# Two ordering edges and one moved load at the hand-over from attention to the first GLU layer

## Chip, cores and metric

One core of a Trainium2 chip; each ratio compares runs of one chip. The metric is the time of one execution on the device in microseconds (us), median of several.

## The reference, cut to what matters

```python
x = A_x                                             # 2048 tokens x 1024, bf16
x = x + _A_ref(_layernorm(x), A_wqkv, A_wo)         # dilated local attention, 32 heads of 32, window 8
x = x + _B_ref(_layernorm(x), W_gate, W_up, W_down) # relu(x Wg) * (x Wu) @ Wd, 3584 wide
x = x + _A_ref(...); x = x + _B_ref(...)            # the same again
```

## The kernel before: the parts that matter here

The 2048 tokens are worked in 4 blocks of 512, twice, so 8 block steps `n`. TensorE should never wait; VectorE does the attention of a later block while TensorE does the big matmuls of an earlier one. The argument is about one place: attention of block 0 ends, and layer B of block 0 begins. In that stretch TensorE does, in this order, V of blocks 1 and 2 (`acc_v`), the output projection of block 0 (`acc_wo`), V of block 3 (`acc_v`), then the gate and up products of layer B (`acc_g`, `acc_u`).

What must happen between `acc_wo` and `acc_g` for each of the four 128-token tiles t of block 0: VectorE evicts `acc_wo` into x, the tile is normalized (t=0 and 1 on ScalarE, t=2 and 3 on VectorE, the power -0.5 on POOL, the GpSimd engine), and a DMA transpose turns it into `xnT_b`, which every `acc_g` reads whole.

```python
def ln2(n, ats, turn_at=None, dve=()):            # norm in front of layer B
    stats, apply, turn, hold = ln_steps(n, "b", False, dve)
    for t, a in enumerate(ats):
        ev.append((a, stats[t]))
        ev.append((a + 4.0, apply[t]))
        if turn_at is None:
            ev.append((a + 6.5, turn(t)))         # DMA transpose of tile t
    ...
ln2(0, [t_wo0 + 2 * GRP * (t + 1) + 0.1 for t in range(TPB)], None, (2, 3))
```

Events (time, function) are sorted by time and emitted in that order. The times are a plan, not a schedule: the compiler then orders each engine's instructions by itself, and an earlier event has priority. Only the DMAs and the groups of matmuls keep the emitted order, because `sp_dma` and `pe_group` chain each to the previous one with an ordering edge (`tc.issue_after`: an instruction is placed behind another). All DMAs but two loads of x at the start go through one queue.

Weights come in 1 MB slabs through a ring of 5 buffers. A load is emitted when the slab five places earlier in the plan is done:

```python
def slab_events(events):
    for i, (key, src, _) in enumerate(slab_plan):
        ...                                       # f: allocate from the ring, load
        events.append((slab_plan[i - RING][2] + 0.3 if i >= RING else 0.1 * i, f))
```

The plan's order is ..., V (2 slabs), wo (2), g0, u0, g1, u1, g2, ... (g for gate, u for up; these names are used below). The two wo slabs are planned to be done earlier than the two V slabs, so u1 and g2 are emitted before u0 and g1.

The attention of block 1 begins with sums of products q*k on VectorE, 16 products (`t`, the first of each half `ac`) and 14 adds, 2.2 us each:

```python
nc.vector.tensor_tensor(t[:], i0, i1, op=ALU.mult)   # 128 x 2048, f32 out
if c > 1: add(h, c - 1)
...
spread(sums1[:5], t_qk1 + 50.0, 4.4)                 # products 0..4
spread(sums1[5:], t_v3 + 6.0, 4.4)                   # the rest
```

## Time and profile before

Median 1647.76 us of three runs.

| What | Where it shows | us |
|---|---|---|
| TensorE busy | page | 1618.9 of 1646.7 (98%) |
| first acc_wo waits for oT | TensorE waits | 1.7 |
| acc_g waits (called "the pause" below) | TensorE waits | 6.2 |
| from the end of V of block 3 (151.0, where the next group would have started) to the second acc_g | timeline | 12.8, of which 3.45 is work |

The TensorE waits of the kernel before from 60 us to the end (engine, line, what it waited for: us in total, times, longest). These are all its waits in that stretch; the slow clock after the pause comes on top. `issue` means that the profile shows no releaser for the matmul itself; its weight load waited for `xnT_b` (PEld, 6.7 us in the view of that tile):

```profile
PE acc_g L115 <- issue: 6.2, 1, 6.2
PE acc_wo L115 <- DMA oT<-o_d: 1.7, 1, 1.7
PE acc_u L115 <- DMA w_u<-in_B_W_up_dram: 0.5, 1, 0.5
```

The same on the timeline of TensorE (start, duration, what, in brackets the idle time before it):

```profile
123.38 13.99 PE L115 MATMUL acc_wo<-w_o,oT 128*128 128x512 bf16 x62 [1.69 <-DMA oT<-o_d]
137.21 13.98 PE L115 MATMUL acc_v<-xnT_a,w_v 128*128 128x512 bf16 x64
157.38 3.57 PE L115 MATMUL acc_g<-xnT_b,w_g 128*128 128x512 bf16 x8 [6.20 <-issue]
161.48 2.50 PE L115 MATMUL acc_u<-xnT_b,w_u 128*128 128x512 bf16 x8 [0.52 <-DMA w_u<-in_B_W_up_dram]
163.81 1.89 PE L115 MATMUL acc_g<-xnT_b,w_g 128*128 128x512 bf16 x8
```

A group of 8 matmuls takes 1.89 us when all is well, starting every 1.73 us. After the pause the first takes 3.57: the clock is slow.

The DMA queue at the pause, from the timeline of SP (start, time that the issuing took):

```profile
140.31 6.57 SPq L104 DMA_TRANSPOSE xnT_b<-xn_b  x2
146.98 0.53 SPq L104 DMA_DIRECT2D w_u<-in_B_W_up_dram  x1
147.60 0.58 SPq L104 DMA_DIRECT2D w_g<-in_B_W_gate_dram  x1
148.28 7.04 SPq L104 DMA_TRANSPOSE xnT_b<-xn_b  x2
155.42 0.52 SPq L104 DMA_DIRECT2D w_u<-in_B_W_up_dram  x1
```

Here is what to see: transposes 0 and 1, then u1 and g2, then transposes 2 and 3, which took 7 us to issue, then u0, which acc_u waits for.

And VectorE, from its timeline. The first line is the product `ac`, which stands in front of the rest of the softmax of block 0; then the last attention output of block 0, the product just in front of the first eviction of acc_wo, that eviction, and the last norm (t=3):

```profile
79.09 2.28 DVE L411 TENSOR_TENSOR ac<-q,k 128x2048 f32<-128x2048 bf16 x1
...
117.06 0.76 DVE L476 TENSOR_TENSOR ohm<-pv 128x512 bf16<-128x512 bf16 x2
...
129.18 2.29 DVE L411 TENSOR_TENSOR t<-q,k 128x2048 f32<-128x2048 bf16 x1
131.39 1.28 DVE L518 TENSOR_TENSOR x<-acc_wo,x 128x512 bf16<-128x512 f32 x2
...
150.81 0.55 DVE L235 TENSOR_SCALAR xn_b<-x,mv,rstd 128x1024 bf16<-128x1024 bf16 x1 [0.44 <-POOL rstd L262]
```

### The profile page before, as it was taken

What the parts mean: (1) busy time and instruction counts of PE and PEld (TensorE: products, weight loads), DVE (VectorE), ACT (ScalarE), POOL (GpSimd) and SP (SyncE); (2) the same over time, 40 slices, a digit from 0 to 9 for tenths busy, and PEclk for the clock granted to TensorE, in tenths of its full rate; (3) what the DMA queues carried; (4) which work ended last, traced back from release to release, by engine and by line L of the source; (5) the groups of instructions that cost most, each with busy time, mean ns of one, the idle gap of its engine ahead of it and who ended that gap; (6) DMA issues with size and microseconds to landing.
All of it is one profiled execution on the core that took longest, in us unless ns stands there. A gap on an engine that the chain in (4) does not pass through costs nothing.

```text
span 1646.7 us, 18588 instructions
## 1 busy us (share of the span) xinstructions
PE 1618.9 (98%) x7527; PEld 777.7 (47%) x7576; DVE 1058.7 (64%) x918; ACT 511.9 (31%) x1057; POOL 267.0 (16%) x220
## 2 busy tenths in 40 slices
PE   7998999999999999999999999999999999999999
PEld 4543445444454445444454444544445444444444
DVE  3699898978198845949459493694927948211111
ACT  5834412414231522315124151340513411131110
POOL 1322005401052102111052010520105100000000
PEclk9999999999999999999999999999999999999999
DMA  9548766755747475774747748477475774655441
GB/s 295 93 141 229 181 169 189 204 171 164 219 148 208 133 208 156 225 207 142 210 155 203 188 153 230 157 185 204 151 228 178 190 220 151 203 154 183 153 163 68
DMA packets 371222, 296.81 MB, mean 180 GB/s; under 512 B 142400, under 2 KB 351296, under 8 KB 370240
## 3 DMA queue, kind: packets, MB, share of 16 engines
q1 hardware_dynamic: 370848, 295.10, 61.7%
q8 instruction: 59, 0.97, 0.2%
q10 hardware_dynamic: 288, 0.52, 0.1%
q14 instruction: 27, 0.22, 0.0%
HBM read 256.77 MB, written 21.00 MB: 169 GB/s over the span
## 4 chain that ended last, share of the span: by engine, by line
PE 90%; DVE 4%; ACT 3%; DMA 1%; issue 1%; POOL 1%; SPq 0%; ACTq 0%; DVEq 0%; POOLq 0%
PE acc_u L115 24%; PE acc_g L115 23%; PE dacc L115 23%; PE acc_wo L115 6%; PE acc_k L115 5%; PE acc_q L115 5%; PE acc_v L115 4%; DVE pv L473 1%; DMA x<-in_A_x_dram 1%; DVE t L411 1%; DVE pv L474 1%; ACT xn_a L221 0%; ACT xn_a L222 0%; DVE ac L421 0%; DMA w_u<-in_B_W_up_dram 0%
## 5 line engine op out<-in xcount | busy, mean ns | idle before, releaser
L115 PE MATMUL acc_g<-xnT_b,w_g 128*128 128x512 bf16 x1792 | 425.1, 380 | 6.2 <-issue 6.2
L115 PE MATMUL acc_u<-xnT_b,w_u 128*128 128x512 bf16 x1792 | 423.9, 379 | 0.5 <-DMA w_u<-in_B_W_up_dram 0.5
L115 PE MATMUL dacc<-w_d,hT 128*128 128x512 bf16 x1759 | 386.3, 379 | 1.7
L543 DVE TENSOR_TENSOR hT<-acc_u,r 128x512 bf16<-128x512 f32 x224 | 154.1, 690 | 317.4 <-PE acc_u L115 304.6
L542 ACT ACTIVATE r<-acc_g 128x512 bf16<-128x512 f32 x224 | 132.6, 594 | 704.9 <-PE acc_g L115 702.0
L115 PEld LDWEIGHTS <-w_g 128*128 128x128 bf16 x1792 | 175.0, 98 | 220.2 <-DMA xnT_b<-xn_b 6.7
L115 PEld LDWEIGHTS <-w_u 128*128 128x128 bf16 x1792 | 175.4, 98 | 213.1 <-DMA w_u<-in_B_W_up_dram 1.4
L115 PEld LDWEIGHTS <-hT 128*128 128x128 bf16 x1792 | 175.3, 98 | 211.4
L411 DVE TENSOR_TENSOR t<-q,k 128x2048 f32<-128x2048 bf16 x98 | 223.7, 2290 | 10.0 <-ACT k L354 7.0
L421 DVE TENSOR_TENSOR ac<-ac,t 128x2048 f32<-128x2048 f32 x84 | 192.0, 2286 | 0.4
L359 POOL COPY kh<-k 128x14 bf16<-128x14 bf16 x64 | 85.9, 1347 | 449.7 <-ACT k L354 449.7
L570 DVE TENSOR_TENSOR x<-dacc,x 128x512 bf16<-128x512 f32 x64 | 42.5, 688 | 164.6 <-PE dacc L115 164.6
L473 DVE TENSOR_TENSOR pv<-a,vhm 128x4096 bf16<-128x4096 bf16 x64 | 145.6, 2289 | 0.0
L226 POOL TENSOR_TENSOR st_b<-st_b,neg_half 128x1 f32<-128x1 f32 x30 | 62.7, 2095 | 325.2 <-ACT st_b L225 325.2
L115 PE MATMUL acc_wo<-w_o,oT 128*128 128x512 bf16 x496 | 111.0, 379 | 2.5 <-DMA oT<-o_d 1.7
L226 POOL TENSOR_TENSOR st_a<-st_a,neg_half 128x1 f32<-128x1 f32 x32 | 44.0, 1376 | 339.8 <-ACT st_a L225 339.8
L115 PEld LDWEIGHTS <-oT 128*128 128x128 bf16 x512 | 50.0, 98 | 62.2 <-DMA oT<-o_d 2.2
L474 DVE TENSOR_TENSOR pv<-pv 128x2048 bf16<-128x2048 bf16 x64 | 77.9, 1222 | 0.2
L358 POOL COPY k<-kh 128x14 bf16<-128x14 bf16 x48 | 67.5, 1406 | 53.4 <-DVE t L411 53.4
L221 ACT ACTIVATE xn_b<-x 128x1024 bf16<-128x1024 bf16 x30 | 31.3, 1045 | 93.9 <-DVE x L518 93.9
L350 ACT CAST q<-acc_q 128x512 bf16<-128x512 f32 x64 | 37.3, 583 | 68.5 <-PE acc_q L115 68.5
L315 ACT CAST vT<-acc_v 128x512 bf16<-128x512 f32 x64 | 36.9, 586 | 66.5 <-PE acc_v L115 66.5
(123 smaller groups left out, 1178.1 us busy)
## 6 DMA issues: line engine op xcount, KB each, us to landing
w_g<-in_B_W_gate_dram SPq DMA_DIRECT2D x56, 1024.0 KB, 6.4
w_u<-in_B_W_up_dram SPq DMA_DIRECT2D x56, 1024.0 KB, 5.2
w_d<-in_B_W_down_dram SPq DMA_DIRECT2D x48, 1024.0 KB, 5.8
w_o<-in_A_wo_dram SPq DMA_DIRECT2D x16, 1024.0 KB, 7.2
vhm<-v_d SPq DMA_DIRECT2D x32, 284.0 KB, 6.9
v_d<-vT SPq DMA_DIRECT2D x8, 1024.0 KB, 9.7
oT<-o_d SPq DMA_DIRECT2D x32, 256.0 KB, 4.2
w_d<-in_B_W_down_dram SPq DMA_DIRECT2D x16, 512.0 KB, 3.8
```

The source lines that it names most:

```text
L115: tail_pe[0] = nc.tensor.matmul(*args, **kwargs).ins
L226: nc.gpsimd.tensor_tensor(rstd, vpe, neg_half[:, 0:1], op=ALU.pow)
L350: nc.scalar.copy(q[:], acc[:])
L358: nc.gpsimd.tensor_copy(k[:, 0:HALO], khalo[n - 1][:, c, :])
L359: nc.gpsimd.tensor_copy(khalo[n][:, c, :], k[:, BLK:BLK + HALO])
L411: nc.vector.tensor_tensor(t[:], i0, i1, op=ALU.mult)
L421: nc.vector.tensor_tensor(o, ac[:], t[:], op=ALU.add)
L473: nc.vector.tensor_tensor(tt[:], a_bc, v_sh, op=ALU.mult)
L474: nc.vector.tensor_tensor(tt[:, 0:4], tt[:, 0:4], tt[:, 4:8], op=ALU.add)
L542: nc.scalar.activation(r[:], acc[:], ACT.Relu)
L543: nc.vector.tensor_tensor(hold["hT"][:, j, :], accs["u"][:], r[:], op=ALU.mult)
L570: nc.vector.tensor_tensor(xs, ac[t], xs, op=ALU.add)
```

## The change

Its intent: the products of block 1 shall not run in front of work that the hand-over waits for. Products 0 to 4 are held by an ordering edge behind the last attention output of block 0, and the rest behind the norm of t=3. The last transpose is emitted 1 us later and the others 0.5 us earlier, so that the load of u0 goes in front of the last one. The norm of block 3 is emitted 10 us later.

```diff
+    gate = [None]
@@ apply(t), norm on VectorE
-                    nc.vector.tensor_scalar(hold["xn"][:, t, :], ..., op0=ALU.subtract, op1=ALU.mult)
+                    gate[0] = nc.vector.tensor_scalar(hold["xn"][:, t, :], ..., op0=ALU.subtract, op1=ALU.mult).ins
@@ prod_sum_steps
-                nc.vector.tensor_tensor(t[:], i0, i1, op=ALU.mult)
+                if n == 1:
+                    with tc.issue_after(gate[0]):
+                        nc.vector.tensor_tensor(t[:], i0, i1, op=ALU.mult)
+                else:
+                    nc.vector.tensor_tensor(t[:], i0, i1, op=ALU.mult)
@@ pv_steps
-                nc.vector.tensor_tensor(ohm[:, ...], tt[:, 0], tt[:, 1], op=ALU.add)
+                gate[0] = nc.vector.tensor_tensor(ohm[:, ...], tt[:, 0], tt[:, 1], op=ALU.add).ins
@@ ln2
-                ev.append((a + 6.5, turn(t)))
+                ev.append((a + (7.5 if t == TPB - 1 else 6.0), turn(t)))
@@
-    ln1(3, 66.0, t_v2 + 9.5, True, 5.0)
+    ln1(3, t_qk1 + 12.0, t_v2 + 9.5, True, 5.0)
-    spread(sums1[5:], t_v3 + 6.0, 4.4)
+    spread(sums1[5:], t_v3 + 5.0, 4.4)
```

## The prediction

> **What bounds the kernel.** TensorE: 98% busy on the page, 90% of the chain that ended last. After the start-up its list of waits holds two losses that matter:
>
> - 1.69 us at 121.7 us: the first acc_wo waits for oT, the attention output read back (timeline of TensorE).
> - The pause at 151.0 us: V of block 3 is done, acc_g starts at 157.38 (6.2 us idle; the weight load waits for xnT_b, the normalized, transposed input). acc_g then takes 3.57 us instead of 1.89; acc_u waits 0.5 us for w_u. The granted clock was 0.60 in 157.4 to 164 (windows). The Trainium skill ("TensorE: Matmul & The Clock Gate", section "Part 1: The HAM clock gate") says the clock halves after an idle window of about 3.4 us; the trace agrees (about 2.5 us lost after this pause, none after the 1.69 us one). The second acc_g starts at 163.81; without the pause: 151.0 + 3.45 = 154.5. Loss 9.3 us.
>
> Together about 11 us, 0.7%.
>
> **What the change does.** Nothing is added or removed; VectorE order and DMA issue order change.
>
> 1. The first product (ac, 2.2 us at 79.09) stood before reciprocal, a and pv of block 0. Held behind the last pv it leaves pv 2.2 us earlier (end 117.7 to 115.5), and oT too: the 1.69 us pause goes.
> 2. Products 5 and on are held behind the last normalization on VectorE (t=3). It ran at 150.81; without two products and an add ahead of it I expect 142 to 145.
> 3. The load of the first w_u moves ahead of the last transpose in the one DMA queue. Issued at 155.42, landed 161.43; now issued near 147 to 150.
> 4. The norm of block 3, emitted 10 us later, already filled ScalarE's idle time: nothing.
>
> **How much is on the critical path.** The queue is the catch. In the trace two 1 MB loads (w_u, w_g at 146.98 and 147.60) go between transposes 1 and 2. Transpose 2, issued at 148.28, took 8.1 us to land, and transpose 3 landed right behind it at 157.35 although its input was ready at 151.36. So the pause was bounded by transpose 1, whose input comes from ScalarE's norm of t=1 (ready 145.6), plus 2.5 MB of queue. That norm hangs on the evictions of acc_wo and moves by only 2 to 4 us. A third 1 MB load, about 3 us at this window's 350 GB/s, now stands before transpose 3. So transpose 3 lands at 154 to 158 instead of 157.35; w_u no longer waits (0.5 to 1 us). The 1.7 us won at acc_wo partly become a longer pause. Net gain about 3 us; if the ScalarE norms come 5 us earlier, 8; if only 2, none.
>
> Later: the sums of block 1, wanted near 208.8, ended near 200; VectorE goes on with them in the pause, so they stay in time.
>
> **Prediction.** 1644.5 us, 8 in 10 within 1638.5 to 1649.0. Faster by over 2%: 0.01; within 2%: 0.98; slower: 0.01.
>
> **What would show it.** Timeline of VectorE: no ac between ssum and rs; pv ends near 115.5. TensorE waits: none of acc_wo for oT; acc_g still waits for xnT_b, 4 to 8 us, and starts cold; acc_u waits for nothing. The first w_u is issued before the last transpose. Second acc_g at 158 to 164.
>
> **What would make it wrong.** The compiler orders VectorE or ScalarE otherwise: acc_wo evicted at once would bring transposes 0 and 1 forward by 5 us or more, the queue would drain before V of block 3 ends, and nearly all 11 us would be won. Or the products held back come late for the logits at 208.8 and TensorE stalls there.

## The result, and the profile after

| Kernel | Median us | Runs | Ratio to before (95%) |
|---|---|---|---|
| before | 1648.04 | 4 | |
| after | 1650.80 | 4 | 1.0015 (0.9998 to 1.0032) |

Ratios here and below are the mean time of one kernel's runs over that of the other's of the same rounds, so not quite the ratio of the medians quoted. The sign is wrong: about 2.5 us slower (0.15%) where 3 us faster was predicted, and 1650.8 lies above the range that ended at 1649.0. The interval alone barely includes 1; the traces and the experiment e2 below settle the sign.

The TensorE waits of the kernel after, from 60 us to the end:

```profile
PE acc_g L118 <- issue: 11.0, 1, 11.0
PE acc_wo L118 <- DVE x L525: 0.2, 1, 0.2
```

The wait for oT and the wait for w_u are gone, as intended. The pause grew from 6.2 to 11.0 us. On the timeline of TensorE:

```profile
121.08 10.52 PE L118 MATMUL acc_wo<-w_o,oT 128*128 128x512 bf16 x48
...
135.26 14.17 PE L118 MATMUL acc_v<-xnT_a,w_v 128*128 128x512 bf16 x64
160.44 3.57 PE L118 MATMUL acc_g<-xnT_b,w_g 128*128 128x512 bf16 x8 [11.01 <-issue]
163.81 2.38 PE L118 MATMUL acc_u<-xnT_b,w_u 128*128 128x512 bf16 x8
166.02 1.89 PE L118 MATMUL acc_g<-xnT_b,w_g 128*128 128x512 bf16 x8
```

The second acc_g starts 2.2 us later than before (166.02 against 163.81), and the span is 2.2 us longer (1648.9 against 1646.7): everything after is the old trace, shifted. The DMA queue, timeline of SP:

```profile
139.99 6.57 SPq L107 DMA_TRANSPOSE xnT_b<-xn_b  x2
146.65 0.53 SPq L107 DMA_DIRECT2D w_u<-in_B_W_up_dram  x1
147.27 0.59 SPq L107 DMA_DIRECT2D w_g<-in_B_W_gate_dram  x1
147.96 4.41 SPq L107 DMA_TRANSPOSE xnT_b<-xn_b  x1
152.49 0.51 SPq L107 DMA_DIRECT2D w_u<-in_B_W_up_dram  x1
153.10 2.85 SPq L107 DMA_TRANSPOSE xnT_b<-xn_b  x1
```

u0 now stands in front of transpose 3. Transpose 3 started to issue at 153.10 and TensorE went on 7.3 us later. Its input had been ready since 146.31, by the last line here (VectorE; the lines answer to those shown of before):

```profile
114.55 0.74 DVE L483 TENSOR_TENSOR ohm<-pv 128x512 bf16<-128x512 bf16 x2
115.22 2.28 DVE L416 TENSOR_TENSOR ac<-q,k 128x2048 f32<-128x2048 bf16 x1
...
128.87 2.29 DVE L416 TENSOR_TENSOR t<-q,k 128x2048 f32<-128x2048 bf16 x1
131.08 1.28 DVE L525 TENSOR_TENSOR x<-acc_wo,x 128x512 bf16<-128x512 f32 x2
...
145.76 0.55 DVE L238 TENSOR_SCALAR xn_b<-x,mv,rstd 128x1024 bf16<-128x1024 bf16 x1 [0.66 <-POOL rstd L265]
```

The attention output ends 2.5 us earlier and the last norm 5 us earlier. But the first eviction of acc_wo is only 0.31 us earlier: `ac` now stands between attention and eviction, and the 2.5 us are spent there.

### The profile page after: what moved, and what is told of

The parts are those of the page before. It is cut to its first block, busy times and chain, and to the rows that moved or that the text cites. A ratio compares the mean times of both kernels' runs of the same rounds, so it can differ in the third digit from the quotient of the medians.

```text
span 1648.9 us, 18636 instructions
## 1 busy us (share of the span) xinstructions
PE 1620.7 (98%) x7576; PEld 777.8 (47%) x7576; DVE 1059.4 (64%) x918; ACT 512.2 (31%) x1057; POOL 267.3 (16%) x220
## 4 chain that ended last, share of the span: by engine, by line
PE 91%; DVE 3%; ACT 3%; DMA 1%; issue 1%; POOL 1%; SPq 0%; DVEq 0%; ACTq 0%; POOLq 0%
PE acc_g L118 24%; PE acc_u L118 23%; PE dacc L118 23%; PE acc_wo L118 6%; PE acc_k L118 5%; PE acc_q L118 5%; PE acc_v L118 4%; DVE pv L480 1%; DMA x<-in_A_x_dram 1%; DVE pv L481 1%; DVE t L416 1%; DMA xnT_b<-xn_b 1%; ACT xn_a L224 0%; ACT xn_a L225 0%; ACT xn_a L241 0%
## 5 line engine op out<-in xcount | busy, mean ns | idle before, releaser
L118 PEld LDWEIGHTS <-w_g 128*128 128x128 bf16 x1792 | 175.0, 98 | 225.0 <-issue 16.1
L418 DVE TENSOR_TENSOR t<-q,k 128x2048 f32<-128x2048 bf16 x84 | 191.8, 2290 | 9.7 <-ACT k L357 7.0
L229 POOL TENSOR_TENSOR st_a<-st_a,neg_half 128x1 f32<-128x1 f32 x32 | 48.0, 1499 | 339.6 <-ACT st_a L228 339.6
L361 POOL COPY k<-kh 128x14 bf16<-128x14 bf16 x48 | 63.8, 1328 | 60.2 <-DVE t L418 43.8
```

Of the source, the lines that this page charges most:

```text
L118: tail_pe[0] = nc.tensor.matmul(*args, **kwargs).ins
L229: nc.gpsimd.tensor_tensor(rstd, vpe, neg_half[:, 0:1], op=ALU.pow)
L361: nc.gpsimd.tensor_copy(k[:, 0:HALO], khalo[n - 1][:, c, :])
```

## The experiments

Theory Q, formed from these traces: the pause is bounded by the one DMA queue. Transpose 1 is its start (it hardly moved), and each 1 MB load between it and transpose 3 adds about 3 us. The change put in a third one. Rivals: V, the held products cost the time by their order on VectorE; N, the norms bound the pause, not the queue.

A comparison of the order of the instructions showed which experiments are clean. The later emission of the norm of block 3 was not run alone, since compiled alone it gave the order of before on all engines; that compilation is not on record, but in the traces ScalarE's order in before and after is the same up to 160 us. The rest can be read from the traces: e1 and before have the same DMA order, e1 and after the same order on every engine and differ in the DMAs alone; e2 and before the same VectorE order (ScalarE differs in a few places after the pause); e4 and after differ in the DMA order alone; e12 and e11 in the place of one POOL instruction. The moment at which acc_wo starts varies by up to 1.7 us between profiles in which it does not wait for oT (120.15 in e1, 121.81 in e3), so the traces are compared by the length of the pause rather than by absolute times.

| Run | Median us | Ratio to before (95%) | Pause, us |
|---|---|---|---|
| e1: edges, old DMA order | 1647.61 | 0.9997 (0.9983 to 1.0010) | 7.8 |
| e2: no edges, new DMA order | 1651.27 | 1.0017 (1.0004 to 1.0029) | 9.5 |
| e3: edges, 1 MB ahead of transpose 3 | 1646.25 | 0.9979 (0.9965 to 0.9992) | 6.0 |
| e4: edges, needed loads first | 1640.70 | 0.9953 (0.9940 to 0.9965) | 2.0 |
| e5: no edges, needed loads first | 1643.86 | 0.9974 (0.9962 to 0.9987) | 3.6 |
| e8: first edge only, needed loads first | 1643.88 | 0.9973 (0.9960 to 0.9987) | 3.1 |
| e9: second edge only, needed loads first | 1641.03 | 0.9951 (0.9938 to 0.9963) | 0.8 |
| e7: after, products 3 and on behind the norm | 1650.94 | 1.0012 (1.0000 to 1.0025) | 4.6 |
| e6: e4, products 3 and on behind the norm | 1649.69 | 1.0003 (0.9990 to 1.0015) | none |
| e10: e4, products 4 and on, logits later | 1641.18 | 0.9957 (0.9945 to 0.9970) | none |
| e11: e6, logits later | 1643.10 | 0.9970 (0.9957 to 0.9982) | none |
| e12: e11, one POOL copy moved | 1638.72 | 0.9943 (0.9929 to 0.9956) | 0.3 |

Each has 5 runs against 9 of before on the same chip; all gave correct results.

### e1 and e2: which half of the change costs the time

e1 is the kernel after with `ev.append((a + 6.5, turn(t)))` as before. e2 is the kernel before with only

```diff
-                ev.append((a + 6.5, turn(t)))
+                ev.append((a + (7.5 if t == TPB - 1 else 6.0), turn(t)))
```

> The change with the transposes at their old places, so that the first w_u load goes behind the last transpose again; VectorE order as after the change. Theory Q (the one DMA queue bounds the pause, and the third 1 MB load in front of the last transpose made it longer): last transpose lands near 157.0, acc_u waits for w_u again by 0.5 to 1 us, second acc_g near 163.4, time 1647.5 +- 0.8, like before. Rival V (the held products cost the time, by VectorE order): the loss stays, 1650.5 +- 0.8.

> The kernel before with nothing but the new places of the transposes. Q: w_u is issued before the last transpose, which lands near 160.4; acc_u does not wait; second acc_g near 166, time 1650.3 +- 0.8, so the whole loss of the change without its edges. V: 1648.0 +- 0.8, as before.

Measured: 1647.61 and 1651.27 us (e2 0.2 us over its margin). The whole loss goes with the DMA order; the rival V falls. In e1 the 1.7 us gained at oT reappear as a pause longer by 1.6 us (7.8 against 6.2). So by themselves the edges bring nothing, because the pause ends when the transposes land, whenever it starts.

### e3, e4, e5: the loads in front of the last transpose

A table of emission times is put over those of the plan:

```diff
-            events.append((slab_plan[i - RING][2] + 0.3 if i >= RING else 0.1 * i, f))
+            at = slab_plan[i - RING][2] + 0.3 if i >= RING else 0.1 * i
+            events.append((SLAB_AT.get(key, at), f))
+    # e3: u1, g2 behind the last transpose
+    SLAB_AT = {("u", 0, 1): 142.1, ("g", 0, 2): 142.2}
+    # e4 (on after), e5 (on before): also u0, g1 as soon as acc_wo has freed the buffers
+    SLAB_AT = {("u", 0, 0): 129.8, ("g", 0, 1): 129.9, ("u", 0, 1): 142.1, ("g", 0, 2): 142.2}
```

> The change, with the two loads needed later (second w_u, third w_g) moved behind the last transpose; the first w_u stays in front of it. So 1 MB lies in the queue ahead of the last transpose, where the kernel after has 3, e1 has 2 and e4 has 0. Theory Q, about 3 us for each MB: transpose 1 goes out near 145.3 as in after, last transpose lands near 153.5 to 154.5, second acc_g near 159.6, time 1644.4 +- 1.5. If only the newly inserted load counted and not the other two: as after, 1650.8.

> The change, with the first w_u and second w_g loaded as soon as acc_wo is done, before transpose 0, and the two loads needed later (second w_u, third w_g) behind the last transpose. Only the order of DMA issues differs from the kernel after. Q: the two loads run while the queue is empty, transpose 1 goes out near 145.3, transpose 3 near 147 to 149 and lands near 151; pause about 2 us instead of 11 and no slow clock; second acc_g near 155; 1639.5 +- 1.5. Rival N (the norms on ScalarE and VectorE bound the pause, not the queue): second acc_g stays above 163, time above 1647.

> The same DMA order on the kernel before, without the edges. Q with the edges useful once the queue is free: the last norm on VectorE stays at 150.8, transpose 3 lands near 154.5, second acc_g at 158 to 160.5, time 1643 +- 1.5: better than before, but 3 to 5 us behind e4. If the edges are worth nothing even then: equal to e4 within 1 us.

Measured: 1646.25 (0.4 us over the stated margin; in its profile acc_wo started late, at 121.81), 1640.70 and 1643.86 us. The queue of e4 and what TensorE then did (timelines of SP and TensorE):

```profile
133.45 0.37 SPq L107 DMA_DIRECT2D w_u<-in_B_W_up_dram  x1
135.18 0.37 SPq L107 DMA_DIRECT2D w_g<-in_B_W_gate_dram  x1
139.71 9.34 SPq L107 DMA_TRANSPOSE xnT_b<-xn_b  x4
```

```profile
151.14 3.53 PE L118 MATMUL acc_g<-xnT_b,w_g 128*128 128x512 bf16 x8 [1.98 <-DMA xnT_b<-xn_b]
154.46 1.98 PE L118 MATMUL acc_u<-xnT_b,w_u 128*128 128x512 bf16 x8
156.28 1.89 PE L118 MATMUL acc_g<-xnT_b,w_g 128*128 128x512 bf16 x8
```

The same bytes are moved; only the order is other. The pause fell from 11.0 to 2.0 us, and N falls for the kernel after: the norms are ready at nearly the same moments as there (145.02 for t=1, 146.04 for t=3, each 0.3 us earlier). One expectation failed: the clock was slow even after this short pause (acc_g took 3.53 us; see the last section).

With all the kernels the effect of the queue can be read off. The table gives the time from the end of the norm of t=1 on ScalarE, which releases transpose 1, to the restart of TensorE:

| Kernel | MB between transposes 1 and 3 | t=1 ready | acc_g starts | difference |
|---|---|---|---|---|
| after | 3 | 145.30 | 160.44 | 15.1 |
| e2 | 3 | 145.37 | 160.35 | 15.0 |
| e7 | 3 | 138.71 | 153.73 | 15.0 |
| before | 2 | 145.62 | 157.38 | 11.8 |
| e1 | 2 | 144.39 | 156.31 | 11.9 |
| e3 | 1 | 146.04 | 156.13 | 10.1 |
| e4 | 0 | 145.02 | 151.14 | 6.1 |

Each MB costs 2 to 4 us, 3 on average (15.1 - 6.1 over 3). In e4, too, it is the norm of t=1 that counts: transposes 1, 2 and 3 were issued one behind the other at 145.05, 146.37 and 147.76, the last landed 3.25 us later, and the norm of t=3 was ready at 146.04, in time for its turn. In e5, without the second edge, it was not: t=3 was ready at 150.8, its transpose was issued at 150.80, and TensorE restarted at 154.09. So once the queue is free, the norms do bound the pause. In before and e2 the norm of t=3 is ready at 151.4 and 151.1, in after and e1 at 146.3 and 145.4; within each pair of the same order this made no difference. The Trainium skill ("DMA: Bandwidth & Descriptors", section "Queues, rings and completion order") says that on each DMA engine descriptors are consumed in ring order; in after, transpose 2 landed at 156.2, behind the last load in front of it, which landed at 155.3.

### e8 and e9: which edge is worth something, once the queue is free

With the DMA order of e4, one edge at a time:

```diff
-                if n == 1:
+                if n == 1 and h == 0 and c < 5:        # e8: first edge only
+                if n == 1 and (h, c) >= (0, 5):        # e9: second edge only
```

> e4 without the second edge; the first stays. Theory: the second edge is what gains in e4. Last norm on VectorE near 149.8 as in the kernel before, last transpose lands near 153, pause near 4 us with a slow clock, second acc_g near 158.5, time 1643.3 +- 1, that is e5 within 1 us. If the first edge is worth something by itself: below 1642.2.

> e4 without the first edge: the product ac is free to run in the softmax of block 0 again; the second edge stays. The 1.6 us wait for oT comes back, V of block 3 ends near 151, the last transpose lands near 151.2 as in e4: pause under 1 us, no slow clock, second acc_g near 154.7, time 1639.2 +- 1, equal to e4 or better. So the first edge would be worth nothing or less, all the gain of e4 over e5 coming from the second. If the first edge is worth its 1.7 us: 1642.3.

Measured: 1643.88 and 1641.03 us (e9 0.8 us over its margin). With e5 and e4 this makes a square of ratios: no edge 0.9974, first 0.9973, second 0.9951, both 0.9953. The first edge is worth nothing, the second about 0.2%, 3 to 4 us. Why the first is worth nothing, in e9: acc_wo waits 1.5 us for oT as before, V of block 3 ends 1.8 us later, and the last transpose lands only 0.6 us later than in e4 (151.64 against 151.00). The pause is 0.8 us then, without a slow clock, instead of 2.0 us with one. In e8 the last norm is back at 150.8 us, and TensorE also waited 1.8 us for an eviction of V that stood late on ScalarE; why was not looked into, but it does not explain the missing gain, since the pause ended at 154.10, where it ended in e5 (154.09).

### e7 and e6: the evictions at once

The prediction named a second way out: evict acc_wo at once. To try it, fewer products go in front of the norm:

```diff
-    spread(sums1[:5], t_qk1 + 50.0, 4.4)
-    spread(sums1[5:], t_v3 + 5.0, 4.4)
+    spread(sums1[:3], t_qk1 + 50.0, 4.4)
+    spread(sums1[3:], t_v3 + 5.0, 3.7)
```

e7 is that on the kernel after, e6 on e4.

> The kernel after with the same split, and its DMA order kept. This is the other half of what the prediction named: evictions at once, transposes 0 and 1 earlier. Theory: transpose 1 goes out near 138 instead of 145.3, the queue of 3 MB then runs from 139 on, last transpose lands near 151 to 153, pause 2 to 4 us with a slow clock, second acc_g 156.5 to 158.5, time 1642 +- 2. If transposes 0 and 1 do not matter for the pause: 1650.8.

> e4, with only products 0 to 2 before the norm and products 3 and on held behind it. It asks what is left of the pause in e4 (2.0 us and a slow clock). Theory: acc_wo of t=0 is evicted late because a product (t_4) stands in front of it on VectorE, which delays ScalarE's norms. With t_3 and t_4 behind the norm: first eviction near 126.5 instead of 130.8, transpose 3 landed by 143, no pause and no slow clock after V of block 3, second acc_g near 152.8, 1637.0 +- 1.2; the sums of block 1 end near 200 to 204, still in time. Rival: the rest of the pause has another cause (landing of a load, latency), time as e4, 1640.7.

Measured: 1650.94 and 1649.69 us. The time of e7 is that of its rival, yet not for the rival's reason; e6 missed both of its numbers, being 9 us slower than e4. In e7 the pause shrank as expected, to 4.6 us, with the second acc_g at 159.92 (after: 166.02); both are a little over what was expected. In e6 it is gone: the timeline has no idle time between V of block 3 and acc_g. The gain is given back later. The TensorE waits of e6 from 60 to 260 us:

```profile
PE L L118 <- DVE s L430: 4.4, 1, 4.4
PE acc_u L118 <- ACT r L551: 4.1, 1, 4.1
```

The first is at the logits of block 1 (207.48 us): the sums came late, because VectorE was idle for several us between 129 and 141 while products waited behind the edge. e7 has that wait too (4.5 us). The second is at 175.0. ScalarE stood for 7.0 us at a norm of block 2, waiting for a power on POOL, and POOL's timeline in e6 shows why:

```profile
167.83 2.12 POOL L363 COPY k<-kh 128x14 bf16<-128x14 bf16 x1 [27.31 <-DVE ac L418]
169.91 3.19 POOL L231 TENSOR_TENSOR st_a<-st_a,neg_half 128x1 f32<-128x1 f32 x2
```

A small copy, needed only for block 2, stood in front of the powers and waited for a held product (`ac`). After each of the two stalls the next group took about 3.6 us instead of 1.9, the slow clock again.

### e11, e10, e12: taking the two new stalls away

e11 is e6 with the logits, softmax and pv of block 1 placed later:

```diff
-    ev.append((t_gu0 + 48.1, red1)); ev.append((t_gu0 + 48.2, lambda: softmax(1)))
+    ev.append((t_gu0 + 55.1, red1)); ev.append((t_gu0 + 55.2, lambda: softmax(1)))
-            spread(pv_steps(1), at + 58.0, 5.5)
+            spread(pv_steps(1), at + 64.0, 5.5)
```

e10 is the same with four products in front of the norm (`sums1[:4]`, the rest 4.0 apart). e12 is e11 with the first copy of block 2 ordered behind the powers:

```diff
+                last_pow[0] = nc.gpsimd.tensor_tensor(rstd, vpe, ..., op=ALU.pow).ins
+                    elif n == 2:
+                        with tc.issue_after(last_pow[0]):
+                            nc.gpsimd.tensor_copy(k[:, 0:HALO], khalo[n - 1][:, c, :])
```

> e6 with only the logits and pv of block 1 placed later, as in e10. Theory: e6 lost 4.4 us at the logits, about 2 us more by the slow clock after it, and 4.1 us plus 2 us near 171. Only the first part goes: 1643.5 +- 1.5, stall near 171 still there. If the loss of e6 had another cause: 1649.7.

> e4 with product t_4 moved behind the norm (4 products before it instead of 5), and the logits and pv of block 1 placed 7 and 6 us later on their engines, to give VectorE the time that the held products need. Theory: first eviction near 128.5 to 130, last transpose landed before V of block 3 ends at 149.2, no pause, and no stall at the logits: 1636.5 +- 1.5. If the POOL stall that e6 showed near 170 (norm of block 2 behind a copy that waits for the held products) returns: 1640 to 1643.

> e11 with one instruction moved: on POOL the first k<-kh copy, which waits for a held product, goes behind the four st_a powers of the norm of block 2 instead of in front of them. Nothing else changes on any engine. Theory: that copy held up the powers, they held up ScalarE, and ScalarE the r that TensorE waited for near 171. So the 4.1 us stall and about 2 us of slow clock go, 1637.2 +- 1.5, the fastest of all. If the copy was not the cause: 1643.1, as e11.

Measured: e11 1643.10, e10 1641.18, e12 1638.72 us. e11 and e12 met their theories, e12 at the very edge of its margin. e10 missed its first number and met the second. The compiler pulled an add into the place of the held product, and the first eviction came at 131.54 instead of 128.5 to 130; there was no pause all the same. But the POOL stall came back, as the second number supposed: the same copy, done at 166.56 when `ac` was there, stood in front of the powers, and ScalarE stood for 8.3 us. Between 164 and 176 us TensorE had four small waits for `r` and `hT` (2.8 us together); which of them the stall caused was not tested. With one POOL instruction moved, the waits of TensorE in e12 from 60 to 1640 us are:

```profile
PE acc_g L119 <- DVE hT L556: 1.1, 1, 1.1
PE acc_g L119 <- DMA xnT_b<-xn_b: 0.3, 1, 0.3
```

and POOL does the powers before any copy:

```profile
164.30 2.08 POOL L232 TENSOR_TENSOR st_a<-st_a,neg_half 128x1 f32<-128x1 f32 x2 [23.22 <-ACT st_a L231]
```

e12 is the fastest version found, 0.57% faster than before by the ratio; 1638.72 against the 1650.80 of after, 12 us.

## Why the prediction was wrong

- **What bounds the kernel: right.** Two losses of 1.69 and 9.3 us; e12, in which both are gone but for 0.3 us, is 9.5 us faster by the medians (1648.19 and 1638.72 of its rounds), against the "about 11 us" named.
- **oT comes earlier and its wait goes: right.** pv ended 2.5 us earlier (2.2 predicted), no wait for oT.
- **The last norm at 142 to 145: right in kind**, it started at 145.76 instead of 150.81. It had no effect, since the queue and not this norm bounded the pause. That was in the prediction, too.
- **The third load adds about 3 us: right**, 15.1 against 11.8 us in the table of the queue. **w_u no longer waits: right**, 0.5 us gained.
- **The failing step:** "That norm hangs on the evictions of acc_wo and moves by only 2 to 4 us." The norm of t=1 moved by 0.3 us (ready at 145.62 before, at 145.30 after; timeline of ScalarE, before and after):

```profile
144.38 1.24 ACT L238 ACTIVATE xn_b<-x,st_b 128x1024 bf16<-128x1024 bf16 x1
144.06 1.24 ACT L241 ACTIVATE xn_b<-x,st_b 128x1024 bf16<-128x1024 bf16 x1
```

  I let the evictions follow the earlier end of pv. But `ac` had only moved: it now ran between pv and the evictions, and since the compiler still put t_4 in front of the first one, seven products and adds stood there instead of six. 2.5 us were gained in front of pv and 2.2 spent behind it. e7 shows that these products set the norm: with two of them behind the last norm, the first eviction came at 126.61 instead of 131.08 and t=1 was ready at 138.71. The prediction also said that with only 2 us nothing would be gained; with 0.3 us the third load turned that into a loss.
- **A second error, of addition:** even with 2 to 4 us and a load of 3 us, transpose 3 lands at 157.35 - (2 to 4) + 3, that is 156.4 to 158.4, and not at "154 to 158". With the 0.3 us that were measured the same sum gives 160.1; TensorE restarted at 160.4. The terms were there, and a gain was assumed on top of them.
- **The norm of block 3 emitted later: not tested alone**; up to 160 us ScalarE's order in the traces of before and after is the same.
- **The sums stay in time: right** for this change (the last ended at 204.0, the logits started at 211.0). In e6 the last sum ended at 207.4, and TensorE, without the pause, came to the logits at 202.7 already: there it broke.
- **"acc_wo evicted at once ... nearly all 11 us would be won": wrong as stated.** e7 did nearly that (t=1 ready 6.6 us earlier): the queue did not drain in time (pause 4.6 us), and the products held for it came late. It takes the queue, the evictions, the logits and the POOL order together (e12).

## What to carry to other kernels

Where all DMAs share a queue, count the bytes between the transfer that an engine waits for and the last event that releases the queue: here each 1 MB prefetch in front cost 3 us, and ordering loads by when they are needed was worth more than the ordering edges (e5 and e1). Holding an operation back does not remove it: ask what stands in its new place, and which other engine has an instruction that waits for it in front of work that is needed sooner. When a wait at the start of a stretch is removed, look first at what ends the stretch, for if that doesn't move, the gain turns into a longer wait there.

## What the Trainium skill lacked or had wrong

- "TensorE: Matmul & The Clock Gate", section "Part 1: The HAM clock gate": it gives one idle window of about 3.4 us, free-running, before the clock halves. In e4 a pause of 1.98 us was enough. Windows of e4 (columns: stretch, length, busy us of the engines with counts, granted clock, DMA share, GB/s):

```profile
149.00:152.00 3.00, 1.02 (x4) 0.37 (x4) 3.00 (x2) 0.89 (x1) 0.00 (x0) 0.87 0.91 197
152.00:154.00 2.00, 2.00 (x6) 0.64 (x5) 1.90 (x2) 1.78 (x5) 0.00 (x0) 0.50 1.09 376
154.00:156.00 2.00, 2.00 (x9) 0.88 (x8) 2.00 (x2) 1.29 (x4) 0.00 (x0) 0.84 1.06 340
```

  The clock was 1.00 up to 151 and 0.61 from 151 to 152, so it fell about 2 us after TensorE had stopped at 149.16 (an estimate from these windows). The pause of 1.69 us in before, and that of 0.84 us in e9, cost no clock. A limit between 1.7 and 2.0 us isn't shown by this; that it depends on how the pause falls in the window isn't shown either.
- "DMA: Bandwidth & Descriptors", section "DMA Transpose (X-bar)": it has no time for issuing a small transpose behind other transfers. The transposes of 128x1024 bf16 landed in 3.0 us when the queue was empty and in 8.3 us behind two loads of 1 MB (both in after); issuing took 1.23 us, or 4.41 us behind the loads, and in that time nothing else was issued from that queue.
